# Hashed attention by whole head pairs instead of half pairs, ahead of a PReLU MLP

## The chip, the core and the metric

The kernel runs on one core of a Trainium2 chip. The metric is the device time of one execution in microseconds, as a median over runs. A profile shows one execution, with every instruction of the five engines: TensorE (PE, with its weight loads as PEld), VectorE (DVE), ScalarE (ACT), GpSimd (POOL) and SyncE (SP), which here issues most DMA transfers.

## The reference

Four batches of eight heads, 768 positions, head dimension 64. A query sees only the keys that fall into its own bucket: six signs of a projection make the bucket number. The result, turned to 3072 tokens of 512 features, goes through a two-layer MLP of width 2048 with a learned slope for negative values. All data is float32.

```python
q_bits = (np.einsum('bhsd,dk->bhsk', q, proj) > 0)          # k_bits likewise, 6 bits
mask = q_bucket[:, :, :, None] == k_bucket[:, :, None, :]
scores = np.where(mask, scale * np.matmul(q, k.transpose(0, 1, 3, 2)), -1e9)
attn = np.exp(scores - scores.max(axis=-1, keepdims=True))
attn = attn / (attn.sum(axis=-1, keepdims=True) + 1e-9)
x = np.matmul(attn, v)                                      # -> (3072, 512)
h = x @ w_in
out = (np.maximum(h, 0) + alpha * np.minimum(h, 0)) @ w_out
```

## The kernel before

Two parts follow each other. In the attention (up to about 345 us) a head pair, two heads side by side on 64 partitions each, is worked on at a time; there are 16 pairs. In the MLP (the rest) each batch is a chain of products of blocks, each product cut into seven smaller ones with sums and differences before and after (`Product`, `ff1`, `ff2`).

A pair's 768 queries are two chunks of 384. A **unit** is one chunk of one pair, so there are 32 units. Scores are computed turned: keys on the partitions, queries along the free axis. For one unit that takes six tiles, one per 128 keys, each 2 heads x 384 queries wide. `scores` (L728) makes three of them per call; each tile is two bf16 matmuls of the bucket bits, which give wrong buckets a large negative score, and two float32 matmuls of q and k on top, then one exponential on ScalarE into a buffer `pt`. No maximum is subtracted. `pts` is a ring of ten such buffers, each with a last column of ones.

`attend` (L763) multiplies the six `pt` tiles of a unit with v, in four groups of 32 columns of the array at once, into the PSUM bank `av`. The sum of every query's weights comes another way: VectorE and one DMA transfer add the six tiles up first, and `totals` (L776) sums over the partitions with a matmul of ones into another bank, `sm`:

```python
def add_first(u):
    accp[u] = pool.tile([P, 2, CW], F32, name=f"accp{u}", tag="accp")
    do(DVE.tensor_tensor(accp[u], p(u, 0), p(u, 1), op=ALU.add))
    nc.gpsimd.dma_start(accp[u], p(u, 2), accum_op=ALU.add)
```

`add_last` adds tiles 3 to 5 into `accd`, `add_total` adds `accp`, which needs the transfer to have landed. `divide` (L786) turns the sums with VectorE, takes the reciprocals (`rr`), lets GpSimd copy them across partitions, turns them back (`dn`) and writes x = (av + a small multiple of v's sum) x dn, which SP stores to DRAM.

[...] three buffers of two banks for scores, turned tiles and hash bits (`two_banks`, tag `sc`), one bank `av` and one bank `sm`. The MLP uses the last two again for its banks c and b.

Beside this, each unit treats one piece of the MLP's weights (32 pieces): `weight_abs` on ScalarE; `weight_clamp`, `weight_parts`, `weight_sum` and up to one of the `weight_sums` on VectorE; loads and stores on SP. `hash_bits` of the next pair falls into a pair's first unit, `turn` (128x128 transposes of q and k of the pair after next) into its second, and so do `magnitude` (squares on ScalarE, for a range check) and the loads of q, k and v.

Each engine runs its instructions in the order in which the program gives them (`do`), so the order of the loop over units sets what waits behind what. Only the DMAs' places are left to a scheduler. The first and second half of a unit's score tiles are interleaved with the unit before: unit u's loop body computes `scores(u, 1)` and `scores(u + 1, 0)`, then `divide(u - 1)`, the adds of u, the first add of u + 1, and only then `attend(u)` and `totals(u)`.

```python
scores(u, 1)
if u < last:
    scores(u + 1, 0)
if u:
    divide(u - 1, weight_rest)
load_weight(u + 3)
add_last(u)
add_total(u)
```

The MLP's first weights (`load_w`) and the first batch's x (`load_x`) are loaded together in unit 18, x's differences (`sum_x`) are taken in units 20 to 23.

Of the kernel before, what the change touches and what calls it, by code (L numbers as in the profile page):

```python
# [406 lines left out]
def fast_path(  # L407
# [41 lines left out]
    attn = ctx.enter_context(ExitStack())  # L449
    pool = attn.enter_context(tc.tile_pool(name="sb", bufs=2))  # L450
# [3 lines left out]
    UNITS = NPAIR * NCH  # L454
# [4 lines left out]
    ones = const.tile([P, 32], F32, name="ones")  # L459
# [17 lines left out]
    NPT = 10  # L477
    pts = [pool.tile([P, 2, CW + 1], F32, name=f"pt{i}", bufs=1) for i in range(NPT)]
    n_pt = [0]

    nat, tr, bits = {}, {}, {}
    prob, accp, accd, av, vsum, sums = {}, {}, {}, {}, {}, {}
# [21 lines left out]
    def setup():  # L504

        zero = pool.tile([P, 512], BF16, name="zero", bufs=1)
        do(DVE.memset(zero, 0.0))
        do(DVE.memset(wh, 0.0))
        for s in range(2):
            nc.sync.dma_start(wh[D * s : D * s + D, :NB], proj)  # L510
        nc.sync.dma_start(alpha16, moe_alpha.rearrange("(t p) -> t p", p=P))
        make_identity(nc, ident)
        do(DVE.memset(ones, 1.0))

        ps = psum.tile([P, 512], F32, name="nil", tag="av")
        nil.append(lambda: do(PE.matmul(ps, zero[:, :P], zero, start=True, stop=True)))
        for i in range(7):
            nil[0]()

        do(DVE.memset(hb, 0.0))  # L520
        for r in range(0, P, 32):
            do(DVE.memset(hb[r : r + 2 * NB], 1.0 if r % D else -1.0))
            do(DVE.memset(hb[r : r + NB], -1e-37))

        do(DVE.tensor_scalar(hb_k[:, 0:1], hb, -1.0, None, op0=ALU.mult))
        do(DVE.memset(hb_k[:, 1:2], 0.0))
        for r in range(0, P, 32):
            do(DVE.memset(hb_k[r : r + 2 * NB, 1:2], 0.5))
        for t in pts:
            do(POOL.memset(t[:, :, CW : CW + 1], 1.0))  # L530
        for t in qbs:
            do(POOL.memset(t, 0.0))
# [158 lines left out]
    def hash_bits(pi, halves=BOTH, engine=None):  # L691
# [7 lines left out]
        ps["q"] = psum.tile([P, 1, 512], F32, name=f"hsq{pi}", tag="sm") if engine is DVE else ps["k"]  # L699
# [28 lines left out]
    def scores(u, half):  # L728
        pi, g = divmod(u, NCH)
        qs = slice(g * CW, (g + 1) * CW)  # L730
        for kc in range(half * NC // 2, (half + 1) * NC // 2):
            sc = two_banks(f"sc{u}_{kc}")
            ks = slice(kc * P, (kc + 1) * P)
            for what, first in ((bits, True), (tr, False)):
                for s in range(2):
                    r = slice(D * s, D * s + D)
                    do(PE.matmul(  # L737
                        sc[:, s, :CW], what["k", pi][r, ks], what["q", pi][r, qs], start=first, stop=not first,
                    ))
            pt = pts[n_pt[0] % NPT]  # L740
            n_pt[0] += 1
            do(ACT.activation(pt[:, :, :CW], sc[:, :, :CW], AF.Exp, scale=SCALE / DOWN))  # L742
            prob[u, kc] = pt


    def p(u, kc):
        return prob[u, kc][:, :, :CW]

    def add_first(u):
        accp[u] = pool.tile([P, 2, CW], F32, name=f"accp{u}", tag="accp")  # L750
        do(DVE.tensor_tensor(accp[u], p(u, 0), p(u, 1), op=ALU.add))  # L751
        nc.gpsimd.dma_start(accp[u], p(u, 2), accum_op=ALU.add)  # L752

    def add_last(u):
        accd[u] = pool.tile([P, 2, CW], F32, name=f"accd{u}", tag="accd", bufs=1)
        do(DVE.tensor_tensor(accd[u], p(u, 3), p(u, 4), op=ALU.add))  # L756
        do(DVE.tensor_tensor(accd[u], accd[u], p(u, 5), op=ALU.add))  # L757

    def add_total(u):
        do(DVE.tensor_tensor(accd[u], accd[u], accp[u], op=ALU.add))  # L760


    def attend(u):  # L763
        pi, g = divmod(u, NCH)
        av[u] = psum.tile([P, 512], F32, name=f"av{u}", tag="av")
        w = CW + 1 if g == 0 else CW
        for kc in range(NC):
            for s in range(2):
                for t in range(0, D, 32):
                    do(PE.matmul(  # L770
                        av[u][D * s + t : D * s + t + 32, :w], nat["v", pi][:, s, kc * D + t : kc * D + t + 32],
                        prob[u, kc][:, s, :w], start=(kc == 0), stop=(kc == NC - 1),
                    ))


    def totals(u):  # L776

        sums[u] = psum.tile([P, HW2], F32, name=f"sm{u}", tag="sm")
        for s in range(2):
            for h in range(2):  # L780
                r = D * s + 32 * h
                do(PE.matmul(  # L782
                    sums[u][r : r + 32], ones, accd[u][:, s, h * HW2 : (h + 1) * HW2], start=True, stop=True,
                ))

    def divide(u, between=lambda: None):  # L786

        pi, g = divmod(u, NCH)  # L790
        b, hp = pairs[pi]
        if g == 0:
            vsum[pi] = pool.tile([P, 1], F32, name=f"vs{pi}", tag="vs")
            do(DVE.tensor_scalar(vsum[pi], av[u][:, CW : CW + 1], EPS, None, op0=ALU.mult))
        n = HW2 // 32
        a = pool.tile([P, HW2], F32, name=f"st{u}", tag="st", bufs=1)
        r = pool.tile([P, n], F32, name=f"rc{u}", tag="rc")
        rr = pool.tile([P, 2, n], F32, name=f"rr{u}", tag="rr")
        d = pool.tile([P, CW], F32, name=f"dn{u}", tag="dn", bufs=1)
        do(DVE.transpose(a, sums[u]))  # L800
        do(DVE.tensor_scalar(r, a.rearrange("p (n w) -> p n w", w=32)[:, :, 0], S * EPS, None, op0=ALU.add))
        do(DVE.reciprocal(rr, r.unsqueeze(1).to_broadcast([P, 2, n])))  # L802
        for q0 in (0, D):
            q1 = q0 + 32
            do(POOL.tensor_copy(rr[q0 : q0 + 32, 1], rr[q1 : q1 + 32, 1]))  # L805
            do(POOL.tensor_copy(rr[q1 : q1 + 32, 0], rr[q0 : q0 + 32, 0]))  # L806
        between()
        do(DVE.transpose(d, rr.rearrange("p h n -> p (h n)").unsqueeze(2).to_broadcast([P, 2 * n, 32])))

        x = mid.tile([P, CW], F32, name=f"x{u}", tag="x")  # L810
        do(DVE.scalar_tensor_tensor(x, av[u][:, :CW], vsum[pi], d, op0=ALU.add, op1=ALU.mult))  # L811
        nc.sync.dma_start(x_s[b, hp][:, g * CW : (g + 1) * CW], x)
# [4 lines left out]
    def load_x(b):  # L817
        for m, kh, ch in ((0, 0, 0), (1, 1, 0), (2, 1, 1), (5, 0, 1)):
# [19 lines left out]
    class Product:  # L838
# [9 lines left out]
        def times(self, bank, left, right, start):  # L848

            if start:  # L850
# [3 lines left out]
                else:  # L854
                    t = psum.tile([P, 512], F32, name=self.name + bank, tag="sm" if bank == "b" else "av")
# [217 lines left out]
    def verdict():  # L1073
        ps = psum.tile([4, P], F32, name="vd", tag="sm")
# [15 lines left out]

    last = UNITS - 1
    first, second = slice(0, 1), slice(1, 2)
    load_part(0, "q", slice(0, CH), nc.sync)
# [19 lines left out]
    scores(0, 0)  # L1113
# [3 lines left out]
    add_first(0)  # L1117
# [4 lines left out]
    weight_sum(0)  # L1122
    for u in range(UNITS):
        pi, g = divmod(u, NCH)

        def weight_rest():
            weight_sum(u)
            weight_group(u)
            weight_clamp(u + 1)

        scores(u, 1)
        if u < last:
            scores(u + 1, 0)
        if u:
            divide(u - 1, weight_rest)
        load_weight(u + 3)
        add_last(u)
        add_total(u)
        if u < last:
            add_first(u + 1)  # L1140
            if u == 0:
                weight_abs(1, DVE)
                weight_clamp(1)
        else:
            now = ff1(0, 0)
            now.step(1)
            now.step(5)
        if g == 0 and pi + 1 < NPAIR:
            hash_bits(pi + 1)
        if g == 1 and pi + 2 < NPAIR:  # L1150
            turn(pi + 2, "q")
            turn(pi + 2, "k")
        if u < last:
            weight_parts(u + 1)
        weight_sums(1)
        attend(u)
        totals(u)
        if u == last:
            divide(u)
        if g == 1 and pi + 2 < NPAIR:  # L1160
            load(pi + 2, "v")
        if u == HW + 2:
            load_w(0)
            load_w(1)
            load_x(0)
        if u == HW + 9:
            load_w(2)
        if HW + 4 <= u < HW + 8:
            sum_x(0, u - HW - 4, DVE)
        if u + 2 < NW:  # L1170
            weight_abs(u + 2)
        if u == 1:
            setup_alpha()
        if g == 1:
            for name in "qk":
                magnitude(pi, name)
                if pi + 3 < NPAIR:
                    load(pi + 3, name)


    late = []
    attn.close()
    late.append(ctx.enter_context(tc.tile_pool(name="late", bufs=2)))
# [91 lines left out]
```

## Time and profile before

| what | us |
|---|---|
| median of 3 runs (lowest, highest) | 899.89 (899.43, 901.15) |
| the profiled execution, its own time | 899.33 |
| its span, first to last instruction | 897.5 |
| attention, up to the last sums (L782) | 345.5 |
| exponentials, 192 on ScalarE | 153.6 busy, 0.813 each |
| adding transfers accp, 32 of 384 KB, median to landing | 5.2 |

The page gives each engine's busy time and the costliest groups of instructions with what ended the idle time ahead of them. A float32 matmul stands in the trace as two records with a weight load each, so the 24 v products of a unit are 48 records. Records of matmuls overlap: their starts, not their lengths, give the rate. The times in the timeline and in windows count from the span's start.

### The profile page before, as it was taken

The page shows a single profiled execution, that of the slowest core. Times are in us where ns is not written, and L with a number is a line of the kernel's source. Part 1 is how long each engine was busy: PE and PEld are TensorE (multiplying, and loading weights), DVE is VectorE, ACT ScalarE, POOL GpSimd, SP SyncE. Part 2 cuts the span into 40 slices and gives each one's busy share as a digit, 9 for nine tenths or more (in the row PEclk, how much of TensorE's full clock was granted, in tenths as well). Part 3 has the DMA queues.
Part 4 walks back from the last instruction along what each step waited for, and adds up shares of the span by engine and source line. Part 5 has one row for each costly group of instructions (what it writes and reads, how often), then busy time and mean ns, then how long its engine had stood idle before and what let it go on. Part 6 is the DMA issues. An engine that isn't in the chain of part 4 may idle for free.

```text
span 897.5 us, 15668 instructions
## 1 busy us (share of the span) xinstructions
PE 886.4 (99%) x5886; PEld 590.7 (66%) x5886; DVE 757.3 (84%) x1362; ACT 406.2 (45%) x726; POOL 100.4 (11%) x194
## 2 busy tenths in 40 slices
PE   9999999999999999999999999999999999999996
PEld 4444445444444445557997557997557998556996
DVE  5988988988999996899988668988668989768986
ACT  6788888888888863222112222112222111222111
POOL 1222222222232222120000000000000000000000
PEclk9999999999999999999999999999999999999999
DMA  9778888699799765478333535343525242530242
GB/s 240 183 179 184 209 222 214 169 269 275 170 233 212 186 159 175 174 275 304 123 130 99 171 98 179 101 152 86 173 97 192 95 158 78 155 120 0 95 144 71
DMA packets 131909, 146.88 MB, mean 164 GB/s; under 512 B 78304, under 2 KB 118000, under 8 KB 128240
## 3 DMA queue, kind: packets, MB, share of 16 engines
q1 hardware_dynamic: 118672, 123.90, 44.5%
q0 software_dynamic: 11008, 20.97, 11.7%
q8 instruction: 48, 0.79, 0.4%
q10 hardware_dynamic: 2144, 0.92, 0.4%
q14 instruction: 37, 0.30, 0.1%
HBM read 104.87 MB, written 28.31 MB: 148 GB/s over the span
## 4 chain that ended last, share of the span: by engine, by line
PE 89%; DVE 7%; DMA 2%; issue 1%; SPq 1%; ACT 0%; DVEq 0%; ACTq 0%
PE sc L737 17%; PE av L770 14%; PE f_0a L858 2%; PE z_3a L858 2%; PE z_6a L858 2%; PE z_5a L858 2%; PE f_2a L858 2%; PE f_1a L858 2%; PE z_2a L858 2%; PE f_3a L858 2%; PE z_7a L858 2%; PE z_1a L858 2%; PE z_4a L858 2%; PE f_7a L858 2%; PE f_6a L858 2%; PE f_5a L858 2%
## 5 line engine op out<-in xcount | busy, mean ns | idle before, releaser
L742 ACT ACTIVATE pt<-sc 128x768 f32<-128x768 f32 x192 | 153.6, 813 | 48.5 <-PE sc L737 46.7
L737 PE MATMUL sc<-qT,kT 64*128 64x384 f32 x768 | 155.2, 482 | 0.0
L770 PE MATMUL av<-pt,vn 128*32 128x384 f32 (+1 forms) x1536 | 130.6, 488 | 0.5 <-DVE x L811 0.5
L770 PEld LDWEIGHTS av<-pt,vn 128*32 128x32 f32 x1536 | 46.6, 109 | 75.7 <-issue 71.1
L737 PEld LDWEIGHTS sc<-qT,kT 64*128 64x128 f32 x768 | 68.2, 188 | 35.8 <-issue 35.6
L911 DVE TENSOR_TENSOR g<-g,g 128x384 f32<-128x384 f32 x128 | 68.4, 555 | 2.2
L737 PE MATMUL sc<-qb,kb 64*128 64x384 bf16 x384 | 63.3, 324 | 0.1
L752 POOL DMA_DIRECT2D accp<-pt x32 | 38.6, 1205 | 194.3 <-issue 78.6
L975 DVE TENSOR_TENSOR gs<-g,gs 128x768 f32<-128x768 f32 x56 | 53.4, 953 | 1.0
L967 DVE TENSOR_TENSOR ws<-wl 128x512 f32<-128x512 f32 x56 | 38.5, 688 | 17.7 <-DMA wl<-w_out_s 16.1
L975 DVE TENSOR_TENSOR gs<-g 128x768 f32<-128x768 f32 x56 | 53.3, 953 | 0.0
L907 DVE SCALAR_TENSOR_TENSOR g<-h,alpha 128x384 f32<-128x384 f32 x32 | 19.7, 616 | 26.4 <-ACT h L900 26.4
L737 PEld LDWEIGHTS <-kb 64*128 64x128 bf16 x384 | 18.8, 94 | 30.6 <-issue 9.2
L760 DVE TENSOR_TENSOR accd<-accd,accp 128x768 f32<-128x768 f32 x32 | 30.7, 958 | 7.7 <-DMA accp<-pt 6.8
L714 ACT ACTIVATE qb<-hs,hb 32x384 bf16<-32x384 f32 x60 | 34.4, 574 | 1.1
L757 DVE TENSOR_TENSOR accd<-accd,pt 128x768 f32<-128x768 f32 x32 | 30.7, 958 | 3.3
L751 DVE TENSOR_TENSOR accp<-pt,pt 128x768 f32<-128x768 f32 x32 | 30.4, 951 | 0.0
L756 DVE TENSOR_TENSOR accd<-pt,pt 128x768 f32<-128x768 f32 x32 | 30.4, 949 | 0.0
L806 POOL COPY rr<-rr 32x6 f32<-32x6 f32 x64 | 27.5, 430 | 2.6
L805 POOL COPY rr<-rr 32x6 f32<-32x6 f32 x64 | 19.8, 310 | 61.6 <-DVE rr L802 60.3
L725 ACT ACTIVATE kb<-hs,hb 64x384 bf16<-64x384 f32 (+1 forms) x45 | 26.0, 578 | 0.6
L800 DVE STREAM_TRANSPOSE st<-sm 128x192 f32<-128x192 f32 x32 | 12.2, 381 | 14.0 <-PE sm L782 13.8
(350 smaller groups left out, 1824.6 us busy)
## 6 DMA issues: line engine op xcount, KB each, us to landing
wi<-w_in_s SPq DMA_DIRECT2D x32, 896.0 KB, 4.7
wl<-w_out_s SPq DMA_DIRECT2D x16, 1024.0 KB, 4.8
accp<-pt POOLq DMA_DIRECT2D x32, 384.0 KB, 5.2
wl<-w_out_r SPq DMA_DIRECT2D x12, 1024.0 KB, 4.9
raw<-in_moe_w_out_dram SPq DMA_DIRECT2D x16, 512.0 KB, 5.2
raw<-in_moe_w_in_dram SPq DMA_DIRECT2D x16, 512.0 KB, 5.0
w_in_s<-wsi SPq DMA_DIRECT2D x16, 448.0 KB, 5.8
vn<-in_v_dram SPq DMA_DIRECT2D x16, 384.0 KB, 6.0
```

Of the source, the lines that this page charges most:

```text
L714: do(ACT.activation(bits["q", pi][D * s : D * s + 32, cols], ps["q"][c : c + 32, 0 if engine is DVE else half, :CW], AF.Sign, bias=hb[c : ...
L737: do(PE.matmul(sc[:, s, :CW], what["k", pi][r, ks], what["q", pi][r, qs], start=first, stop=not first,))
L742: do(ACT.activation(pt[:, :, :CW], sc[:, :, :CW], AF.Exp, scale=SCALE / DOWN))
L751: do(DVE.tensor_tensor(accp[u], p(u, 0), p(u, 1), op=ALU.add))
L752: nc.gpsimd.dma_start(accp[u], p(u, 2), accum_op=ALU.add)
L757: do(DVE.tensor_tensor(accd[u], accd[u], p(u, 5), op=ALU.add))
L760: do(DVE.tensor_tensor(accd[u], accd[u], accp[u], op=ALU.add))
L770: do(PE.matmul(av[u][D * s + t : D * s + t + 32, :w], nat["v", pi][:, s, kc * D + t : kc * D + t + 32], prob[u, kc][:, s, :w], start=(kc = ...
L858: do(PE.matmul(self.ps[bank], self.left(left, k), self.right(right, k), start=start and k == 0, stop=k == self.nk - 1, skip_group_check=no ...
L911: do(DVE.tensor_tensor(new_g(b, to)[:, i], g_m[b, x][:, i], g_m[b, y][:, i], op=ALU.subtract))
L967: do(DVE.tensor_tensor(t, w2[b, n, x], w2[b, n, y], op=op))
L975: do(DVE.tensor_tensor(t, g2[b, n, x], g2[b, n, y], op=ALU.subtract))
```

## The change

The loop runs over 16 pairs instead of 32 units. All twelve score tiles of a pair are made in one go (for pair 0 three of them ahead), key block by key block and both chunks of a block in turn; then come the hash of the next pair, the turns of the pair after next, and v's product of both chunks. `pts` is one set of six buffers, each with both chunks. The adds, the adding transfer, x and its store have twice the width; `accp`, `accd` and x have one buffer each. `av` is two banks, a chunk in each, and the sums go into columns 400 to 495 of the same banks: four matmuls of 192 columns per unit become eight of 96 per chunk, in two accumulating steps, with a pattern of ones that fills 16 of 32 rows at a time. Two weight pieces are treated per pair. The loads of x are spread over four pairs, the MLP's first weight loads over three. The MLP's banks b and c come from a pool that opens once the attention's is closed.

```diff
+    psum_av = attn.enter_context(tc.tile_pool(name="psa", bufs=1, space=bass.MemoryType.PSUM))
-    pts = [pool.tile([P, 2, CW + 1], F32, name=f"pt{i}", bufs=1) for i in range(NPT)]
+    pts = [pool.tile([P, NCH, 2, CW + 1], F32, name=f"pt{i}", bufs=1) for i in range(NC)]
...
+        do(DVE.memset(ones, 0.0))
+        for e in range(2):
+            do(DVE.memset(ones[:, e, 16 * e : 16 * e + 16], 1.0))
...
+    def scores(pi, cells):
+        for kc, g in cells:
...
+            do(ACT.activation(pts[kc][:, g, :, :CW], sc[:, :, :CW], AF.Exp, scale=SCALE / DOWN))
...
+    def add_first(pi):
+        accp[pi] = pool.tile([P, 2 * NCH, CW], F32, name=f"accp{pi}", tag="accp", bufs=1)
+        do(DVE.tensor_tensor(accp[pi], p(0), p(1), op=ALU.add))
+        nc.gpsimd.dma_start(accp[pi], p(2), accum_op=ALU.add)
...
+    def totals(pi):
+        for g in range(NCH):
+            for e in range(2):
+                for s in range(2):
+                    for h in range(2):
+                        r = D * s + 32 * h
+                        do(PE.matmul(
+                            av[pi][r : r + 32, g, SUMS : SUMS + QW], ones[:, e],
+                            accd[pi][:, NCH * g + s, h * HW2 + e * QW : h * HW2 + (e + 1) * QW],
+                            start=e == 0, stop=e == 1, skip_group_check=True,
+                        ))
...
+    for pi in range(NPAIR):
+        i = 2 * pi
+        def weight_begin():
+            weight_clamp(i)
+            weight_parts(i)
+            add_first(pi)
+        scores(pi, [c for c in CELLS if pi or c not in ahead])
+        if pi:
+            divide(pi - 1, weight_begin)
+        else:
+            add_first(pi)
+        weight_sum(i)
+        weight_group(i)
+        load_weight(i + 3)
...
+        weight_clamp(i + 1)
+        add_last(pi)
+        weight_parts(i + 1)
+        weight_sum(i + 1)
+        weight_group(i + 1)
+        load_weight(i + 4)
+        add_total(pi)
+        weight_sums(2)
+        if pi + 1 < NPAIR:
+            hash_bits(pi + 1)
+        if pi + 2 < NPAIR:
+            turn(pi + 2, "q")
+            turn(pi + 2, "k")
+        attend(pi)
+        if pi + 1 == NPAIR:
+            now = ff1(0, 0)
+            now.step(1)
+            now.step(5)
+        totals(pi)
+        if pi + 1 == NPAIR:
+            divide(pi)
+        else:
+            weight_abs(i + 2)
...
+        if pi in (8, 10, 12):
+            load_w((8, 10, 12).index(pi))
+        if 8 <= pi < 12:
+            load_x(0, pi - 8)
+        if pi in (12, 13):
+            sum_x(0, 2 * pi - 24, DVE)
+            sum_x(0, 2 * pi - 23, DVE)
...
+        for name in "qk":
+            magnitude(pi, name)
+            if pi + 3 < NPAIR:
+                load(pi + 3, name)
+        if pi + 1 < NPAIR:
+            weight_abs(i + 3)
```

## The prediction

> **What bounds the kernel now.** I read the page first, then TensorE's waits, then one head pair on TensorE's timeline, then the slack of the other engines beside it. The page's first part:
>
> ```profile
> PE 886.4 (99%) x5886; PEld 590.7 (66%) x5886; DVE 757.3 (84%) x1362; ACT 406.2 (45%) x726; POOL 100.4 (11%) x194
> ```
>
> TensorE is busy in 99% of the span. Its waits, over the whole span, are these five and no more:
>
> ```profile
> PE nil L516 <- DVE hb L520: 1.2, 1, 1.2
> PE sm L782 <- DVE accd L760: 0.9, 1, 0.9
> PE z_2c L858 <- DVE m L996: 0.7, 1, 0.7
> PE av L770 <- DVE x L811: 0.5, 1, 0.5
> PE vd L1075 <- DVE top L1071: 0.3, 1, 0.3
> ```
>
> None lies in the attention between 32 and 345 us: TensorE's own stream sets the time there, and only what shortens that stream, or makes it wait, counts. One pair on its timeline (start, length; 36 rows, cut):
>
> ```profile
> 202.96 0.34 PE L737 MATMUL sc<-qb,kb 64*128 64x384 bf16 x2
> ...
> 207.91 0.51 PE L706 MATMUL hs<-kT,wh 64*32 64x384 f32 x2
> ...
> 208.71 4.09 PE L770 MATMUL av<-pt,vn 128*32 128x385 f32 x48
> 212.62 0.51 PE L782 MATMUL sm<-accd,ones 128*32 128x192 f32 x8
> 213.06 0.34 PE L737 MATMUL sc<-qb,kb 64*128 64x384 bf16 x2
> ...
> 218.01 0.87 PE L678 MATMUL tp_q<-ident,qn 128*128 128x128 f32 x6
> 218.72 0.82 PE L678 MATMUL tp_k<-ident,kn 128*128 128x128 f32 x6
> 219.47 4.08 PE L770 MATMUL av<-pt,vn 128*32 128x384 f32 x48
> 223.36 0.51 PE L782 MATMUL sm<-accd,ones 128*32 128x192 f32 x8
> 223.80 0.34 PE L737 MATMUL sc<-qb,kb 64*128 64x384 bf16 x2
> ```
>
> A pair takes 223.80 - 202.96 = 20.84 us. The same stretch by engine, with the DMA engines' share behind the clock:
>
> ```profile
> 202.96:223.80 20.84, 20.84 (x216) 10.14 (x213) 17.23 (x33) 17.98 (x27) 4.76 (x10) 1.00 0.98 269
> ```
>
> VectorE is busy 17.2 us of it (19.6 in another pair) and ScalarE 18.0: both have room, but little. The DMA engines are nearly full here (0.8 in quieter pairs).
>
> [...] From the starts of single records, a score tile comes every 0.807 us, a round of four v products every 0.3235, a round of sums every 0.163, a transpose every 0.109, a hash round every 0.3225. A pair without switches is 12 x 0.807 + 2 x 0.3225 + 12 x 0.109 + 24 x 0.3235 + 4 x 0.163 = 20.05. The other 0.79 is six switches (scores, hash, v, scores, turns, v; sums share v's mode), 0.131 each. [...] The sums' 192 columns take 163 ns, 3 over the 160 that the 384-column rounds imply. [...] The adding transfer took 4.4 us when quiet and 9.9 while other loads ran[...].
>
> **The change, part by part.** Time t runs from a pair's first score.
>
> *TensorE's order.* One pass per pair leaves scores, hash, turns, v with sums: four switches for six. 2 x 0.131 = 0.26 less per pair.
>
> *Sums.* Sixteen matmuls of 96 columns for eight of 192: eight rounds for four. At half of 160 plus 3, a round is 0.083: 0.664 against 0.652, +0.01. The trace shows no matmul this narrow. The low bound is that; the high bound is a weight load per round, 0.110 as recorded (32 columns): 0.88, +0.22. I take the low one: transposes run at 0.109 though their loads are recorded at 0.14, so a load may end about 0.03 later than its successor starts. Net 0.25 per pair; 15 pairs give 3.75 and the last, where MLP work splits v from sums, one switch: **-3.9**.
>
> *ScalarE.* The same exps, at 0.807 each: the twelfth ends at t=10.8. Signs (4.1), turn copies (1.5), abs, squares and abs (3) end at 19.5. The next pair's first exp is due at 20.6 + 1.1 = 21.7. Its last abs needs the weight load issued at 9.3, which lands in about 5: hidden. Costs nothing with 2 us to spare; a load 6 us late would eat it.
>
> *VectorE.* Widths double. 384 columns take 0.555 (L911), 768 0.953, so 1.04 ns a column: 1536 are 1.75. From the row intervals: sums' transposes and reciprocals to t=1.4, weight clamp and parts 2.1, add_first from 4.4 (fourth exp) to 6.1, dn and x to 8.0, weight sum and clamp to 9.9, add_last two adds to 13.5, weight parts and sum 2.8 to 16.3, add_total to 18.05. v products run from 9.79 + 0.81 + 1.46 = 12.05 to 19.84, so the sums wait for nothing: slack 1.8. The product's banks, now one pair of buffers, must be read (x at 8.0) before v starts at 12.05: free by 4. The one set of probability tiles for two costs nothing while add_total comes before the sums: v, the adds and the transfer have then read it. The weight adds (1.2) and, in two pairs, x's sums (1.9) fall between add_total and the next reciprocals, and are hidden by the wait for the fourth exp.
>
> *The adding transfer*, now 768 KB, is what is late next:
>
> ```profile
> DMA to landing us min/median/max: 4.4/5.2/9.9
> ```
>
> The page gives queue 0 11.7% of 16 engines for 20.97 MB; accp's 12.58 MB of it are 63 us, 2.0 per transfer. So 2.4 are fixed and the rest doubles: 6.4 quiet, 8.0 at the median. GpSimd issues it behind the four copies of the reciprocals, done by 3.4. Issued at t=6.65, it must land by 18.05: 11.4 allowed. Behind it VectorE queues add_total, the weight adds and the next divide; TensorE's sums and all that follows wait for add_total. Stretching all 32 landings as 2.4 + 2 x (L - 2.4), seven exceed 11.4, by 16 us in total: for 16 transfers +8. But those seven ran beside q, k, v loads or weight stores. In the new order these loads are issued from t=-2.7 and, at 9.5 to 12 us from first q issue to last k landing, are nearly over by then; stores run to about 12. I take one pair, where the first MLP loads follow stores (before: 9.9), 2 late, plus odd tenths: **+1.8**, ends 0 and +8.
>
> *Loads.* One x store of twice the size, same bytes. Loads of q and k for a pair are issued at 17.9, the turn that needs them comes 13.3 later (17 before): landing at most 12.2, hidden. SP's order in the built program puts the second MLP weight load right behind the first and the third one x store later, so of the spreading little is left. In SP the x store and next weight load queue behind these.
>
> *Start.* Before, TensorE stood 1.04 before the first sums and 0.7 before the second v (true gaps[...]). Now turns of pair 2 come at 21.6, and its k landed at 23.80: a wait of up to 1.5, and add_total comes by 30 for sums at 32. **-0.3**, from -0.9 to +0.5.
>
> *End.* The MLP's bank b waits for the divide of both chunks: reciprocals 1.4, GpSimd copies 1.0, dn 1.0, x 1.0, 4.5 after the sums, where three MLP products cover 3.98: **+0.5**, up to 2 if VectorE's backlog shows in the next block. It idles 1.5 us there (352.5 to 354).
>
> Sum: -3.9 + 1.8 - 0.3 + 0.5 = -1.9. The profiled execution took 899.33 (span 897.5 and 1.8 around it), so 897.4; the median of the runs, 899.89, lies 0.56 higher: **897.9**.
>
> **Rivals.** (A) *The transfer is late often*: +8 instead of +1.8 gives 904.1. It decides from a landing of 11.4 us. For it: the DMA engines stand at 0.8 to 0.98, and accp, with two buffers, was started a whole unit ahead before, while now it starts and ends within its pair. Against: its place after the loads. At 13 us in every pair it would be 15 x 1.6 - 3.9 = +20, which I hold for rare. (B) *Narrow sums are load-bound*: 16 x 0.22 = 3.5 more, 901.4, no change. For it: two weights alternate; against: the transposes. (C) *No late transfers at all*: 896.1. (D) The load spreading not happening is already in the +1.8.
>
> **Numbers.** A change of 0.2% (1.8 us) is about what a measurement can tell from none: faster below 898.1, slower above 901.7. Forecast with C 0.46 (895.5 to 898.1), partial gains and B 0.27, A 0.27. The forecast lies close to the bound, so half of small slips end in "same". Range 895.5 to 904.5: from C with the start's best to A.
>
> **What would show it.** In the changed profile: a quiet pair at 20.6 us; 32x96 rounds at 0.083 (0.11 means B); the wait "PE sums <- DVE accd" of 0 to 3 us, and behind it "DVE accd <- DMA accp" (8 or more means A); accp's median landing near 8; one wait of 0.5 before f0's b. Any wait of TensorE for ScalarE inside a pair, or a quiet pair above 20.8, makes this prediction wrong.

## The result, and the profile after

The changed kernel took 900.45 us (median of six runs, 899.66 to 902.8), the kernel before 900.18 beside it: 1.0007 times as long [0.9992, 1.0022], so no difference. The forecast was 897.9, in the range 895.5 to 904.5. Run a second time, the changed kernel took 903.76 (901.95 to 905.24) against 899.26: 1.0054 [1.0041, 1.0067]. The profile is of a run of 902.8 us, the longest of the six, so it lost more than the median run did; its span is 901.0.

From the page after, TensorE's share, the total's row, the adding transfer's row and its issue line:

```profile
PE 884.1 (98%) x6142; PEld 597.7 (66%) x6142; DVE 739.9 (82%) x1268; ACT 406.9 (45%) x726; POOL 53.9 (6%) x110
...
L757 DVE TENSOR_TENSOR accd<-accd,accp 128x1536 f32<-128x1536 f32 x16 | 28.1, 1755 | 11.1 <-DMA accp<-pt 11.1
...
L749 POOL DMA_DIRECT2D accp<-pt x16 | 20.6, 1289 | 77.0 <-ACT pt L740 60.5
...
accp<-pt POOLq DMA_DIRECT2D x16, 768.0 KB, 8.8
```

TensorE does 2.3 us less and the span is 3.5 longer: it waits more. VectorE stood 11.1 us for the adding transfer, in four of the 16 pairs. TensorE's waits after:

```profile
PE av L786 <- DVE accd L757: 5.6, 2, 3.9
PE nil L517 <- DVE wh L506: 1.2, 1, 1.2
PE z_2c L871 <- DVE m L1009: 0.7, 1, 0.7
...
PE f_0b L871 <- DVE x L823: 0.3, 1, 0.3
```

The first line is what has grown: before, the sums waited 0.9 us for add_total, once; now they did so twice, 1.76 us in pair 0 and 3.87 in pair 8. A pair without a wait, on TensorE's timeline (start, length):

```profile
136.56 0.34 PE L737 MATMUL sc<-qb,kb 64*128 64x384 bf16 x2
...
147.16 0.87 PE L679 MATMUL tp_q<-ident,qn 128*128 128x128 f32 x6
147.87 0.82 PE L679 MATMUL tp_k<-ident,kn 128*128 128x128 f32 x6
148.62 7.96 PE L770 MATMUL av<-pt,vn 128*32 128x385 f32 x96
156.39 0.85 PE L786 MATMUL av<-accd,ones 128*32 128x96 f32 x32
157.17 0.34 PE L737 MATMUL sc<-qb,kb 64*128 64x384 bf16 x2
```

157.17 - 136.56 = 20.61 us, where it was 20.84. So are pairs 3 to 13 (within 0.05) but for 8 and 9, which took 24.69 and 22.26. The same timeline at pair 8's sums and pair 9's first scores:

```profile
201.68 0.87 PE L786 MATMUL av<-accd,ones 128*32 128x96 f32 x32 [3.87 <-DVE accd L757]
202.48 0.50 PE L737 MATMUL sc<-qb,kb 64*128 64x384 bf16 x2
202.77 1.49 PE L737 MATMUL sc<-qT,kT 64*128 64x384 f32 x4
204.05 0.53 PE L737 MATMUL sc<-qb,kb 64*128 64x384 bf16 x2
204.37 1.49 PE L737 MATMUL sc<-qT,kT 64*128 64x384 f32 x4
...
206.56 0.32 PE L737 MATMUL sc<-qb,kb 64*128 64x384 bf16 x2
```

After the wait the first two score tiles take 1.6 us each instead of 0.81. The stretch view (busy time of the engines, then granted clock, DMA share, GB/s) says why:

```profile
202.40:205.80 3.40, 3.40 (x22) 1.73 (x16) 3.05 (x12) 1.48 (x2) 1.27 (x4) 0.51 1.14 321
```

TensorE ran at half its clock for 3.41 us. What was late is one adding transfer. Its landing times over the kernel:

```profile
DMA to landing us min/median/max: 7.6/8.8/15.4
```

The 15.4 is pair 8's: GpSimd issued it at 184.44, it landed at 199.84, and VectorE, which had stood for it, began add_total:

```profile
199.86 1.76 DVE L757 TENSOR_TENSOR accd<-accd,accp 128x1536 f32<-128x1536 f32 x1 [5.58 <-DMA accp<-pt]
```

SP's queue in the same stretch shows what the transfer ran beside:

```profile
180.13 4.35 SPq L652 DMA_DIRECT2D w_in_s<-wsi  x4
184.72 2.67 SPq L849 DMA_DIRECT2D wi<-w_in_s  x2
187.48 1.36 SPq L824 DMA_DIRECT2D x_s<-x  x1
188.94 1.51 SPq L568 DMA_DIRECT2D raw<-in_moe_w_in_dram  x1
190.50 1.21 SPq L849 DMA_DIRECT2D wi<-w_in_s  x1
```

Four weight stores, then all three first MLP loads of 896 KB, within 11.6 us of issue. The source asks for these loads in pairs 8, 10 and 12; the program as built issues all three in pair 8.

### The profile page after: what moved, and what is told of

It is laid out like the page before. It is cut to its first block, busy times and chain, and to the rows that moved or that the text cites. A ratio compares the mean times of both kernels' runs of the same rounds, so it can differ in the third digit from the quotient of the medians.

```text
span 901.0 us, 15891 instructions
## 1 busy us (share of the span) xinstructions
PE 884.1 (98%) x6142; PEld 597.7 (66%) x6142; DVE 739.9 (82%) x1268; ACT 406.9 (45%) x726; POOL 53.9 (6%) x110
## 3 DMA queue, kind: packets, MB, share of 16 engines
q0 software_dynamic: 10752, 20.97, 11.6%
## 4 chain that ended last, share of the span: by engine, by line
PE 53%; DVE 6%; issue 1%; DMA 0%; SPq 0%; ACT 0%; DVEq 0%; POOL 0%; ACTq 0%
PE z_3a L871 2%; PE z_6a L871 2%; PE z_5a L871 2%; PE f_2a L871 2%; PE f_1a L871 2%; PE z_7a L871 2%; PE z_2a L871 2%; PE f_3a L871 2%; PE z_4a L871 2%; PE f_0a L871 2%; PE z_1a L871 2%; PE f_7a L871 2%; PE f_6a L871 2%; PE f_5a L871 2%; PE f_4a L871 2%; PE z_2c L871 1%
## 5 line engine op out<-in xcount | busy, mean ns | idle before, releaser
L770 PE MATMUL av<-pt,vn 128*32 128x385 f32 (+1 forms) x1536 | 127.4, 486 | 0.0
L770 PEld LDWEIGHTS av<-pt,vn 128*32 128x32 f32 x1536 | 48.7, 109 | 71.1 <-issue 70.1
L748 DVE TENSOR_TENSOR accp<-pt,pt 128x1536 f32<-128x1536 f32 x16 | 28.1, 1758 | 14.9 <-ACT pt L740 14.9
L757 DVE TENSOR_TENSOR accd<-accd,accp 128x1536 f32<-128x1536 f32 x16 | 28.1, 1755 | 11.1 <-DMA accp<-pt 11.1
L754 DVE TENSOR_TENSOR accd<-accd,pt 128x1536 f32<-128x1536 f32 x16 | 28.1, 1759 | 1.7
L753 DVE TENSOR_TENSOR accd<-pt,pt 128x1536 f32<-128x1536 f32 x16 | 28.0, 1753 | 0.0
L749 POOL DMA_DIRECT2D accp<-pt x16 | 20.6, 1289 | 77.0 <-ACT pt L740 60.5
L584 ACT ACTIVATE wx<-raw 128x512 f32<-128x512 f32 x30 | 21.1, 705 | 6.0 <-DMA raw<-in_moe_w_in_dram 5.9
L814 POOL COPY rr<-rr 32x12 f32<-32x12 f32 x32 | 9.7, 305 | 229.0 <-DVE rr L811 228.4
L871 PE MATMUL f_0a<-x,wi 128*128 128x384 f32 x64 | 23.5, 489 | 0.0
```

Source lines behind the costliest of these rows:

```text
L748: do(DVE.tensor_tensor(accp[pi], p(0), p(1), op=ALU.add))
L753: do(DVE.tensor_tensor(accd[pi], p(3), p(4), op=ALU.add))
L754: do(DVE.tensor_tensor(accd[pi], accd[pi], p(5), op=ALU.add))
L757: do(DVE.tensor_tensor(accd[pi], accd[pi], accp[pi], op=ALU.add))
L770: do(PE.matmul(av[pi][D * s + t : D * s + t + 32, g, :w], nat["v", pi][:, s, kc * D + t : kc * D + t + 32], pts[kc][:, g, s, :w], start=(k ...
L871: do(PE.matmul(self.ps[bank], self.left(left, k), self.right(right, k), start=start and k == 0, stop=k == self.nk - 1, skip_group_check=no ...
```

## The experiments

The theory: the merged pairs save what was forecast, and pair 8's late transfer, with the half clock behind it, gives it back. Rivals: the loss is spread over the pairs (VectorE or ScalarE as the new bound), or another transfer stands right behind this one and takes its place.

**The changed kernel again**, on the chip of the next three experiments (the loads taken apart, the transfer replaced, the first filler).

> The changed kernel once more, beside the next three on the same chip. Burst theory: the two switches saved per pair are there (quiet pair 20.6 us against 20.84, 15 x 0.225 = 3.4 us), and one pair gives them back, because the first MLP weight loads stand right behind four weight stores and the 768 KB adding transfer of that pair lands late. Size theory: every adding transfer at its new place is near its limit and several pairs lose tenths. End theory: the loss sits in the MLP, whose banks and VectorE start later. Expected by the burst theory: 900.2 us (899.5 to 902), pair 8 at 24 to 25 us and pair 9 at 20.6 to 22.3; by the size theory other slow pairs than 8 and 9; by the end theory over 1.5 us more from the end of the attention to the end of the span than before.

903.76 us, above the 899.5 to 902 expected. The profiled run (901.95) shows pair 8 at 25.20, pair 9 at 22.16, a landing of 15.82, a sums wait of 4.28 and the half clock for 3.41; pair 0's wait was absent. No other pair was slow, and from the end of the attention to the end of the span it took 1.46 us more than the kernel before (1.35 in the first profile; the end theory asked for over 1.5). So pair 8 is what recurs.

**The burst of loads taken apart.** `do` puts a load into the written order of the instructions; without it SP's built order has the three loads together. The line makes all of the MLP's weight loads, the later ones too.

```diff
-            nc.sync.dma_start(w_m[n], w_in_s[n % NI])
+            do(nc.sync.dma_start(w_m[n], w_in_s[n % NI]))
```

> One call changed: the MLP weight loads are kept at the place where the loop names them, pairs 8, 10 and 12, instead of all three being issued in pair 8 right behind the weight stores. Burst theory: pair 8 falls to 20.6, pair 9 too, 4.1 + 1.65 = 5.7 us off the profile of the changed kernel, so 894 to 895.5 us. Size theory: pair 8 still waits over 1 us for its transfer and pairs 10 and 12 begin to, so 898 to 900. End theory: nothing, 900.

896.44 us, 0.9965 [0.9952, 0.9978], somewhat above the burst theory's 894 to 895.5. The profiled run is the slowest of the five (899.05). Its landings and its first wait:

```profile
DMA to landing us min/median/max: 7.6/8.8/12.8
```

```profile
PE av L786 <- DVE accd L757: 1.8, 2, 1.3
```

Pair 8's transfer now landed after 12.04 us and its sums waited 0.50; pair 5's, beside four weight stores, an x store and a weight piece, took 12.85 and cost 1.31. There is no half clock in the attention, and pairs 10 and 12, to which the loads moved, both took 20.62. Whether the four faster runs had pair 5's wait too is not on record. The burst made the landing of 15 us; the traffic that was there without it still makes some of 12 to 13.

**The late transfer replaced.** The burst stays; in pair 8 alone VectorE does the add.

```diff
+        if pi == 8:
+            do(DVE.tensor_tensor(accp[pi], accp[pi], p(2), op=ALU.add))
+        else:
             nc.gpsimd.dma_start(accp[pi], p(2), accum_op=ALU.add)
```

> In pair 8 alone VectorE makes the addition that the transfer makes in the other pairs; the loads stay as they are, all in pair 8. If the late transfer is the only thing that the burst delays, pairs 8 and 9 fall to 20.6 and the time to 894.5 to 895.5. If the burst also delays the weight piece that ScalarE reads ahead of the next pair's exponentials (in the profile of the changed kernel that piece landed at 202.35, after the transfer at 199.84, with ScalarE standing in front of it), the wait only moves: TensorE's score tiles of pair 9 stop for their buffers for some 3 us, and the time is 897 to 898.5. End theory: 900.

895.77 us, 0.9958 [0.9946, 0.9971], 8.0 less than the changed kernel on that chip. Every other pair took 20.62, pair 8 20.88, and the attention ended at 340.64 (345.49 in the kernel before). So one transfer out of sixteen makes the difference between the forecast gain and what was measured. ScalarE did stand for its weight piece there:

```profile
197.32 0.67 ACT L584 ACTIVATE wx<-raw 128x512 f32<-128x512 f32 x1 [2.36 <-DMA raw<-in_moe_w_in_dram]
```

But TensorE did not stop for it, so the wait did not move on to ScalarE: with no adding transfer in that pair the piece took 9.7 us to land, and 13.4 in the changed kernel, where ScalarE stood 5.94.

**Is the half clock due to the idle time?** Products of zeros, read by nobody, ahead of pair 8's sums; first 14, then 26.

```diff
     def totals(pi):
+        if pi == 8:
+            fill = two_banks("fill")[:, 0]
+            for n in range(14):
+                do(PE.matmul(fill, zeros[0][:, :P], zeros[0], start=True, stop=True))
```

> In pair 8, ahead of the sums, TensorE runs 14 matmuls of zeros that need nothing, some 3 us, while it would stand waiting for the sums' input. The wait for the transfer is not shortened. If the slow score tiles after the wait (1.6 us each for the first two, 0.81 later) come from the clock that the records show at 0.5 for 3.4 us after a wait of 4 us, they are at 0.81 now, pair 9 takes 20.6 instead of 22.3 and the time falls by 1.6, to 898.6. If they come from ScalarE's late exponentials, pair 9 stays at 22.3 and the time at 900.2.

901.16 us, 1.0018 [1.0008, 1.0027]. In its profile the transfer took 17.37 us, so the sums still waited 2.70 after the filler, the half clock came for 3.41 us, and pair 9 took 22.3, as the other reading (ScalarE's late exponentials) had said. But the filler had not covered the wait, so this settled nothing about the cause, and it was made longer:

> As the run with 14 filler matmuls, but 26 of them (about 5.6 us at 0.21 each, the rate of the shorter filler), so that TensorE never stands idle while pair 8's adding transfer is late. Leaves nothing out; the filler computes zeros that nobody reads. If the half clock after the wait comes from TensorE's idleness: no slice at clock 0.5 in the attention, no sums wait over 0.5 us in pair 8, pair 8 at 20.6 + 5.6 to 26.5 us, and pair 9 back at 20.6 (with the wait it was 22.2). If instead it comes from something else that goes with the late transfer (DMA load, or power): clock 0.5 near 204 us again and pair 9 at 22.2. One look at about 902, whose median isn't the question.

One run took 901.01. The transfer was as late (17.34), but TensorE did not stand still (of the 26 products one record is missing):

```profile
195.78 5.79 PE L1175 MATMUL fill<-zero 128*128 128x512 bf16 x25
201.66 0.87 PE L787 MATMUL av<-accd,ones 128*32 128x96 f32 x32
202.46 0.34 PE L738 MATMUL sc<-qb,kb 64*128 64x384 bf16 x2
202.63 0.81 PE L738 MATMUL sc<-qT,kT 64*128 64x384 f32 x4
203.27 0.33 PE L738 MATMUL sc<-qb,kb 64*128 64x384 bf16 x2
```

Scores come every 0.81 us at once, pair 9 took 20.61 and no slice of the attention is below full clock. So it was TensorE's idleness that went with the half clock, not the load on the DMA engines: their share was 1.07 and 1.15 here around the filler, at full clock, and 1.14 in the changed kernel's half-clock stretch. The spells of half clock lasted 3.41 us, once twice as long (6.83). The length of the wait alone did not decide: behind one of 2.70 us (the shorter filler) the clock was halved, behind one of 2.91 (in the run with half the transfer, below) it was not.

The traces show where the two differ. In the kernel before and the changed one the stretches from where TensorE first has its full clock to the last change of clock are whole multiples of 3.413 us (260 of them before; 58, one at half clock and 202 after), and the spells of the other runs are one or two of them. So in these traces the clock changed at steps of 3.413 us, wherever a wait began. Cut along these steps, the run with the shorter filler and, below it, the run with half the transfer (length, TensorE's busy time first, the clock behind the brackets):

```profile
200.23:203.65 3.42, 1.31 (x38) 1.04 (x40) 2.14 (x4) 0.64 (x1) 0.00 (x0) 1.00 1.12 326
203.65:207.06 3.41, 3.41 (x16) 1.71 (x14) 2.75 (x10) 1.62 (x2) 1.27 (x4) 0.50 0.88 219
```

```profile
196.96:200.38 3.42, 2.28 (x18) 1.04 (x15) 2.95 (x11) 0.00 (x0) 1.26 (x4) 1.00 1.04 403
200.38:203.79 3.41, 1.64 (x14) 1.13 (x15) 0.00 (x0) 3.06 (x5) 0.00 (x0) 1.00 0.78 176
```

Of the 2.70 us, 2.1 fell into one step, and the next step ran at half clock. The 2.91 were split over two steps, 1.1 and 1.8, and neither had one behind it: from 202.15 on a score tile came every 0.81 us. In the changed kernel, cut the same way by the matmuls' records, the step with 2.66 us of idleness at pair 8's sums and the one with 2.45 at the end of the products were followed by half clock; the next longest at full clock, with 1.21 and 1.04, were not. In the run with one more switch a step already at half clock had 1.6 of idleness and was followed by a second one; hence its 6.83. So of two waits of nearly the same length here one cost the half clock and the other did not, by where they fell on the steps.

**What a switch costs.** q's turns ahead of the hash, so five switches per pair instead of four.

```diff
+            if pi + 2 < NPAIR:
+                turn(pi + 2, "q")
             hash_bits(pi + 1)
         if pi + 2 < NPAIR:
-            turn(pi + 2, "q")
             turn(pi + 2, "k")
```

> The changed kernel with q's turns moved ahead of the hash products, so that a pair goes scores, turns, hash, turns, v with sums: five changes of tiling instead of four, the same matmuls. If a change of tiling costs what the prediction put on it (0.131 us, the rest of 0.79 over six): a quiet pair of 20.62 + 0.13 = 20.75, with no wait of TensorE over 0.1 us in it. Rival (the 0.23 per quiet pair came from something else in the merged order, such as fewer stops for another engine, and a switch is free): 20.62. One look; the total is set by pair 8's late transfer as before and isn't the question.

```profile
135.67 0.34 PE L737 MATMUL sc<-qb,kb 64*128 64x384 bf16 x2
...
145.47 0.88 PE L679 MATMUL tp_q<-ident,qn 128*128 128x128 f32 x6
146.27 0.51 PE L707 MATMUL hs<-kT,wh 64*32 64x384 f32 x2
...
147.08 0.88 PE L679 MATMUL tp_k<-ident,kn 128*128 128x128 f32 x6
147.88 7.96 PE L770 MATMUL av<-pt,vn 128*32 128x385 f32 x96
...
156.44 0.34 PE L737 MATMUL sc<-qb,kb 64*128 64x384 bf16 x2
```

20.77 against 20.62, with no wait in it: 0.15 for the switch, near the 0.13 forecast; the rival's 20.62 is out. Two switches at 0.13 to 0.15 are enough for the 0.23 saved per pair. (The one run took 904.3, with pair 8 as late as ever.)

**All adds on VectorE**, no adding transfer left.

> Every pair adds the third piece of probabilities on VectorE (1.75 us) and no adding transfer is left; loads stay in their burst. Theory (the late transfer alone cost the gain; VectorE has 1.8 us of slack per pair): add_total ends near t=19.8, sums start at 19.84, so pairs at 20.6 to 20.9 us and about 895.8 to 899; the DMA engines lose 12.6 MB and the MLP loads land sooner. Rival (VectorE becomes the bound: its queue was 17 to 19.6 us busy per pair, plus 1.75): quiet pairs at 21 or more, sums waiting 0.4 us or more in each of 15 pairs, 902 or more.

904.69 us, 1.0067 [1.0053, 1.008]: the time is the rival's, though quiet pairs, at 20.89, stayed within the theory's 20.6 to 20.9. VectorE in one of them, which began at 136.27:

```profile
142.49 1.76 DVE L749 TENSOR_TENSOR accp<-accp,pt 128x1536 f32<-128x1536 f32 x1
...
154.55 1.75 DVE L757 TENSOR_TENSOR accd<-accd,accp 128x1536 f32<-128x1536 f32 x1
```

add_total starts at t=18.28 and ends at 20.03, while v is done at 19.84 (as in a quiet pair of the changed kernel): the third add and 0.1 between took the slack and 0.2 more. In pairs 13 and 14, where VectorE also adds the MLP's x, the sums waited 1.13 and 2.15, and the pairs were 1.3 and 2.8 longer. VectorE's slack is real but one add wide.

**Half the transfer.** 384 KB by GpSimd, as before, the other half on VectorE (0.96 us).

> Each adding transfer carries half of the piece (384 KB, as in the kernel before) and VectorE adds the other half (768 columns, about 0.9 us); loads stay in their burst. If a transfer's time goes by its bytes (384 KB: 4.4 quiet, 5.2 median; 768 KB: 7.6 and 8.8): median 5 to 6, pair 8's landing at 15.4 - 3.5 = 12 us or less, its sums wait under 1.0 us and no clock of 0.5: 895.3 to 897. Rival (what is late is the queueing behind the burst of loads, not the bytes): pair 8 lands at 14 or more, waits 2.5 or more and loses the clock as in the changed kernel: 899 to 901.

903.37 us, 1.0048 [1.0034, 1.0062]. The landing went by bytes, as the theory had it: 4.5 at the median, 8.95 in pair 8, and no sums wait there. The time did not follow, because of a wait that neither side had named here, though the expectation for pair 8's add on VectorE had (with all adds on VectorE the same wait showed, with 0.67):

```profile
200.74 0.66 ACT L584 ACTIVATE wx<-raw 128x512 f32<-128x512 f32 x1 [5.99 <-DMA raw<-in_moe_w_in_dram]
201.30 5.17 ACT L740 ACTIVATE pt<-sc 128x768 f32<-128x768 f32 x7
202.15 0.34 PE L737 MATMUL sc<-qb,kb 64*128 64x384 bf16 x2 [2.91 <-ACT pt L740]
```

The weight piece that ScalarE reads landed 11.7 us after issue. ScalarE's queue held the next pair's exponentials behind it, and TensorE, out of free score banks, stood 2.91. A second wait (1.82, sums for add_total) came in pair 14, behind x's sums. So in the burst ScalarE's piece is nearly as late as the adding transfer and stands right behind it; only with the transfer away altogether did both waits go.

**Both cures together, then in better order.** Loads spread, and VectorE's add in pairs 5, 8 and 11.

> Two edits of runs already made, put together: MLP's weight loads are issued in the order of the source (not in a burst behind the stores), and pairs 5, 8 and 11, where the transfer landed at 11 us or more, add on VectorE. Theory (late transfers alone): pairs 5, 8 and 11 at 20.6 to 20.9, no sums wait over 0.3 us after pair 0, no clock of 0.5 in the attention, 895.0 to 896: at or below the better of the two single edits (895.77). Rival (another wait, ScalarE for raw or an x of the MLP, stands right behind): a pair of 21.5 or more again and 896.5 or more.

896.6 us, 0.9968 [0.9956, 0.9981]. The trace is as the theory had it: those three pairs 20.9, all others 20.6, the attention over at 340.60, no sums wait. But the median is 0.6 above the theory's bound of 896, and in the rival's range; the profiled run, at 895.66, is the fastest of the six. No third wait is in its attention, and what the other runs lost was not traced.

Then add_total directly after add_last in those pairs, ahead of the second weight parts:

```diff
         add_last(pi)
+        if pi in (5, 8, 11):
+            add_total(pi)
         weight_parts(i + 1)
...
-        add_total(pi)
+        if pi not in (5, 8, 11):
+            add_total(pi)
```

> As the run with spread loads and the adds of pairs 5, 8 and 11 on VectorE, and in those three pairs the total is added right after the last pieces, ahead of the second weight parts. In that run those pairs took 20.89 where others took 20.62, because the third add (1.76 us and 0.1 between) ate VectorE's slack of 1.7 before the sums. With the total 2.6 to 2.8 us earlier all pairs should take 20.62: attention ends near 339.8 (340.6 without this edit), 895.0 to 896.2. Rival (the 0.27 isn't the order of VectorE's queue): those pairs stay at 20.9, 895.8 to 897.

895.09 us, 0.9960 [0.9946, 0.9974], the lowest median; beside the kernel before on its own chip, the run with only pair 8's add on VectorE is as good (0.9958). All pairs took 20.62, and the attention ended at 339.84, as forecast. TensorE's first waits:

```profile
PE nil L517 <- DVE wh L506: 1.2, 1, 1.2
PE z_2c L874 <- DVE m L1012: 0.7, 1, 0.7
PE tp_q L679 <- DMA qn<-in_q_dram: 0.4, 1, 0.4
```

The wait for add_total is gone. This version takes 0.4% less than the kernel before, in the interval given; beside the changed kernel itself it was not measured.

The same in every pair, with no transfers:

> Spread loads, every third piece added on VectorE, no adding transfer, and the total ahead of the second weight parts in every pair. Theory (VectorE's order, not its load, cost 0.27 in each pair of the run with all adds on VectorE): quiet pairs 20.62, no late wait in pair 8 since neither sums nor VectorE wait for a DMA, 895 to 897; the two pairs with the MLP's x sums may still wait 0.5 to 2. Rival (VectorE, now about 19.7 us busy of 20.6, is the bound and its backlog grows): pairs at 20.9 or more, 900 or more.

899.58 us, 1.0005 [0.9998, 1.0012]. Quiet pairs took 20.62, so the order did cost the 0.27; but the total missed both forecasts. In pair 14 v waited 1.76 for x, in pair 15 0.47, and pairs 13 to 15 were 0.6, 1.8 and 0.5 longer than in the version above. VectorE at the end of pair 13 and in pair 14:

```profile
302.65 1.94 DVE L846 TENSOR_TENSOR x<-x,x 128x768 f32<-128x768 f32 x2
...
309.54 1.76 DVE L750 TENSOR_TENSOR accp<-accp,pt 128x1536 f32<-128x1536 f32 x1
311.22 0.97 DVE L820 STREAM_TRANSPOSE dn<-rr 128x768 f32<-128x768 f32 x1
312.23 1.02 DVE L826 SCALAR_TENSOR_TENSOR x<-av,vs,dn 128x768 f32<-128x768 f32 x1
```

With x's sums and the third add in a row, VectorE reads the product's banks too late for the next v. (Against the version above, these three pairs are 2.9 us of the 4.3 between the profiled runs; another 0.9 was lost by the start of pair 1.)

## Why the prediction was right and where it was wrong

The range held, and each mechanism of the sum was there. The forecast's sign did not come: "faster" had 0.46 and no difference is what was measured, because one term was, in the profiled run, three times its size. By the profiled executions (902.8 against 899.33, so +3.5 where -1.9 was said; by the medians it is +0.3, which points to a smaller term in the median run, and +4.5 in the second measurement, which points to a larger one; the sum's median, 899.89 - 1.9, is 898.0 and not 897.9, a slip on which nothing hangs):

- **Switches and sums: right, a little high.** 20.84 - 20.61 = 0.23 per pair against 0.25, so 15 pairs give 3.4 of the 3.9; a switch measured alone was 0.15 (0.131 said). Rounds of the narrow sums came every 0.0825 us (0.083 said): rival B, the weight loads, is out.
- **The adding transfer: the step that failed.** The place was named rightly (the pair where the first MLP loads follow stores, and VectorE's add_total behind it), the size was not: "2 late" was 4.1, and 1.6 more came from the half clock in pair 9, which was not in the working at all: 5.7 for 1.8. Two sub-steps were low. "2.4 fixed and the rest doubles" gave 6.4 for a quiet transfer; it took 7.6, with the median at 8.8 (8.0 said), so 2.6 us were left under the allowed 11.4 and not 3.4 (from 4.4 us for 384 KB and 7.6 for 768, an estimate is 1.2 fixed and 3.2 that doubles). And for the burst the old worst case of 9.9, stretched by that rule to 17.4, was not used, though the 15.4 to 17.4 measured lie right there: the "2 late" stood for a landing of 13.4. The working had already seen that the loads stay together in SP's order.
- **Rival A** (late often, seven pairs, +8) was wrong in its count, though the repeat came out near its time: the landings of 11.4 and 11.0 in pairs 5 and 11 cost nothing, as the bound of 11.4 said.
- **VectorE: right.** The adds took 1.75 and add_total ended at t=18.2 (18.05 said); the slack of 1.7 is what the third add used up.
- **ScalarE "costs nothing": right in quiet pairs, wrong in its cover.** The weight piece was to land "in about 5"; in pair 8 it took 9.6 to 13.9 in the runs where the burst or the adding transfer was left in that pair, and 3.8 to 5.8 where both were away. "A load 6 us late would eat it" is what the half transfer then showed.
- **Start: right by accident.** Of the +2.13 at the attention's end, 5.7 - 3.4 leaves -0.2 for the start (-0.3 said). But k's turn never waited as the working had it; pair 0's own transfer, 11.3 us beside the first loads, put 1.8 in its place: add_total began only at 30.7, where the working had it over by 30. These figures for the start are what is left of the attention's time when the other terms are taken off. Without that wait the start was worth -1.6 (repeat) to -2.2 (best version, where the first exponential also began 0.8 sooner than in the kernel before).
- **End: bank b as said**, +0.45 for 0.5. Another 0.9 came in the span's last part, nearly all after the last matmul, and most of it after the landing of the last store; why was not traced.

For the best version, -3.4 from the switches and -2.2 from the start make the -5.65 of the attention (the -2.2 being the remainder, not a check), and +1.3 came from the end: 895.0 from 899.33, and its profiled run took 894.98.

Left open: how late pair 8's transfer was in the runs that were not profiled, and the repeat's 1.8 us between its profiled run (901.95, mean clock 0.995) and its median (0.993). A second spell of half clock, as seen in the run with one more switch (6.83 us, mean clock 0.993), would fit but is not shown.

## What to carry to other kernels

Merging two tiles to save fixed costs also merges their transfers: the slack per transfer has to be compared with the worst landing of the old trace, stretched by the new size, in the very pair where a burst of other loads falls (9.9 us before, 15.4 to 17.4 after), and not with the median (5.2, then 8.8). A stall of TensorE should be priced with the half clock that can follow it: four of the five waits of 2.70 us or more here had it behind them, at about 1.6 us a spell. A late transfer can be replaced by the engine's own add in just the pairs where it is late; doing so everywhere cost 4.5 us against doing it in three pairs, since VectorE's slack is local too.

## What the runs showed of the hardware

- The clock changed at whole multiples of 3.413 us from where it was first full (260 of them in the kernel before; 58, one at half clock and 202 in the changed kernel). Steps at full clock with 2.1 us (the shorter filler), 2.45 and 2.66 us (the changed kernel) of TensorE standing still were followed by half clock; steps with 1.1 and 1.8 us (half the transfer) were not.
- In mid-kernel, waits of 2.70 (the shorter filler), 3.87 (the changed kernel) and 4.28 us (its repeat) brought spells of 3.41 us, and one of 3.71 (one more switch) brought 6.83; a single spell cost about 1.6 us (pair 9 at 22.26 against 20.61). A wait of 2.91, split over two steps (half the transfer), one of 2.15 (all adds on VectorE) and the shorter ones brought none.
- An accumulating transfer of 768 KB took 7.6 us at the least (the changed kernel) against 4.4 for 384 KB (the kernel before), and beside three loads of 896 KB and four stores 15.4 (the changed kernel) to 17.4 (the shorter filler).
- Matmuls of 96 columns in four column tiles started a round every 0.0825 us in the changed kernel, although each weight load is recorded at 0.110.
